# Wide fifth blocks and idle matmuls in a fused attention and feed-forward kernel

## The chip, the cores and the metric

The kernel runs on one core of a Trainium2 chip. The metric is the device time of one execution in microseconds; the time of a kernel is the median over several runs. A core has TensorE (PE, which takes a block of weights into its array and streams columns past it), VectorE (DVE), ScalarE (ACT), GpSimd (POOL) and SyncE (SP, which issues most DMAs). Each executes its own instructions in program order.

## The reference

Attention over 8 batches x 8 heads, 576 positions, 64 values per head, with a mask in blocks of 64 (a query sees keys of its own block and of earlier ones), followed by a feed-forward layer of 4608 tokens, 512 inputs and 2048 inner values, all in float32:

```python
scores = scale * np.matmul(q, k.transpose(0, 1, 3, 2))
scores = np.where(block_i >= block_j, scores, -1e9)
attn = softmax(scores)                      # row maximum taken off first
x = np.matmul(attn, v)                      # -> (4608, 512)
h = x @ w_in                                # 512 -> 2048
sp = np.maximum(h, 0.0) + np.log1p(np.exp(-np.abs(h)))
out = (h * erf(sp)) @ w_out                 # 2048 -> 512
```

## The kernel before, in words

Every float32 operand of a matmul is split into a float16 high part and a float16 low part, and products are sums of two or three float16 matmuls.

**A head n** (64 of them, batch after batch) goes through these steps. `load_qk` brings its keys and queries, `split_qk` makes their high and low parts and copies them by six DMAs into one of three tiles `qk` of 128 rows and 4 x 576 + 64 columns: four parts of 576 columns (part 0 keys low and high, 1 queries high and low, 2 keys high, 3 queries high), with rows of mask below. `maxes` computes scores `s` (L586) with blocks of 128 queries as weights and keys streaming past, and DVE takes each row's maximum (L590); PE transposes them (`mt`, L620) and a DMA puts them into the tile's row 68. `probs` computes the scores again the other way round, `t` (two matmuls, L638 and L639, into one PSUM bank), with blocks of 128 keys as weights and queries streaming past; ACT takes the exponential into `p32` (L643), and ACT, POOL and DVE split it into `ph` and `pl`. For each pair of heads, `pv` multiplies by the values (`u`, L686; 64 columns of weights a head) and `sums` adds up the rows (`us`, L715; 32 columns of ones). For every four heads, `normalise` turns the reciprocal sums (`rt`, L733; transposes `rb`, L751) and stores `x`.

576 is 4 x 128 + 64. The fifth block of queries in `maxes`, of keys in `probs`, `pv` and `sums`, and of positions in `normalise` therefore has 64 rows or columns, which appear as `r`, `kk` and `min(P, S - j * P)`. Rows 64 to 127 of the fifth block of `p32` are set to zero at the start, and the values `v` come padded with zeros to 640 rows.

**The feed-forward part** starts when the weights are decoded (`decode`, `measure_weights`, `split_weight`, on ACT and DVE, over about the first 200 us) and the first batch's `x` is there. A tile of 256 tokens takes four units; a unit is 48 matmuls of 256 columns (`m_h`, L431), a gate on ACT and DVE, and 24 matmuls of 512 columns (`o`, L446).

**The order.** All steps are tasks of a planner (`Plan`). A task has an engine, a cost in ns, the tasks it depends on, the PSUM or SBUF buffers it takes, and a priority: for a step of slot n roughly n plus a fraction (`merge`). The planner simulates the engines with these costs, always gives a free engine the ready task of the lowest priority, and the order that results is the program order of each engine. There are eight PSUM banks; a task that takes one waits in the plan until one is free. Matmuls on PE are booked with 0.4167 ns a column and a few ns.

**Idle matmuls.** `warm` adds a matmul of a constant onto a bank `b_w` that nobody reads. The list of slot n < 8 holds ten of them, with priority n + 1 to n + 2, so they come behind the slot's other work.

Of the kernel before, what the change touches and what calls it, by code (L numbers as in the profile page):

```python
# [22 lines left out]
DEC0, DECR, SPLIT = (0.5, 6.5), (0.35, 0.4), 0.8  # L23
MOE, STEP = 12.5, 0.93
NPH = 3
BYSUM = 4
PSUM = bass.MemoryType.PSUM

# [188 lines left out]
def tile_attention_moe(ctx: ExitStack, tc: tile.TileContext, qk, v, w, maskrows, sels, out):  # L217
    nc = tc.nc
    B, H, D2, S = qk.shape
# [3 lines left out]
    P = 128  # L223
# [9 lines left out]
    NB = 3  # L233
# [6 lines left out]
    NP = (2, 2)  # L240
    plan = Plan()
    add = plan.add
# [21 lines left out]
    ident = cpool.tile([P, P], F32, name="ident")  # L264
# [30 lines left out]
    def mmns(n, f16=False):  # L295
        return n * 0.4167 + (3 if f16 else 13)
# [162 lines left out]
    qks = [spool.tile([P, 4 * S + 64], F16, name=f"qk{i}") for i in range(NB)]  # L459
    for t in qks:  # L460
        nc.sync.dma_start(t[D : D + 5, 2 * S : 4 * S], maskrows)
    sel = spool.tile([P, 4], F32, name="sel")
    nc.sync.dma_start(sel, sels)

# [9 lines left out]
    ident16 = ident.bitcast(F16)[:, :P]  # L474
# [45 lines left out]
    def part(n, i):  # L520

        return qks[n % NB][:, i * S : (i + 1) * S]

    def Q(n, *names):
        return [("qk", n % NB, i) for i in names]

# [52 lines left out]
    def maxes(n):  # L579

        mx, K, hx = mxs[n % 2], D + 4, token("mx", 2)
        kh, qh = part(n, 2), part(n, 3)

        def mm(s, c0, i, k0, w_):
            r = min(P, S - i * P)
            add("PE", mmns(w_, True), lambda: nc.tensor.matmul(s()[:r, c0 : c0 + w_], lhsT=qh[:K, i * P : i * P + r], rhs=kh[:K, k0 : k0 + w_], start=True, stop=True),  # L586
                r=[*Q(n, "kh", "qh"), hx], w=[s])

        def red(col, s, c0, w_, r=P):
            add("DVE", 145 + 1.07 * w_, lambda: nc.vector.tensor_reduce(out=mx[:r, col : col + 1], in_=s()[:r, c0 : c0 + w_], axis=AX.X, op=ALU.max, negate=True),  # L590
                r=[s], w=[("mx", n % 2, col)])

        def a():
            s = bank(f"s01_{n}")
            mm(s, 0, 0, 0, 256)
            mm(s, 256, 1, 0, 256)
            red(0, s, 0, 128)
            red(1, s, 256, 256)

        def b():  # L600
            s = bank(f"s2_{n}")
            mm(s, 0, 2, 0, 384)
            red(2, s, 0, 384)

        def c():
            s = bank(f"s3_{n}")
            mm(s, 0, 3, 0, 512)
            red(3, s, 0, 512)

        def d(j):  # L610
            s = bank(f"s4_{n}_{j}")
            mm(s, 0, 4, 288 * j, 288)
            red(4 + j, s, 0, 288, 64)

        def e():
            add("DVE", 300, lambda: nc.vector.tensor_tensor(out=mx[:64, 4:5], in0=mx[:64, 4:5], in1=mx[:64, 5:6], op=ALU.min), r=[("mx", n % 2, 5)], w=[("mx", n % 2, 4)])

        def f():
            pt = bank(f"mt{n}")
            add("PE", 60, lambda: nc.tensor.transpose(out=pt()[:5, :P], in_=mx[:, :5], identity=ident), r=[("mx", n % 2, i) for i in range(6)] + [hx], w=[pt])  # L620
            mt = buf("a", [5, P], F16, "mt", f"mt_{n}")
            add("ACT", 255, lambda: nc.scalar.activation(mt(), pt()[:5, :P], AF.Copy, scale=1.0 / 32), r=[pt], w=[mt])
            add("ACT", 60, lambda: nc.scalar.dma_start(qks[n % NB][D + 4 : D + 5, 3 * S :].rearrange("o (i p) -> o i p", p=P), mt()), r=[mt], w=Q(n, "m"), lag=2500.0)

        return [a, b, c, lambda: d(0), lambda: d(1), e], f

    def probs(n, out):

        K = D + 5
        sc = qsc[n // 4]  # L630
        klh, qhl, kh, qh = [part(n, i) for i in range(4)]

        def one(j, q0, w_):
            kk = min(P, S - j * P)
            ks = slice(j * P, j * P + kk)
            s = bank(f"t{j}_{n}_{q0}")

            add("PE", mmns(w_, True), lambda: nc.tensor.matmul(s()[:kk, :w_], lhsT=klh[:, ks], rhs=qhl[:, q0 : q0 + w_], start=True, stop=False), r=Q(n, "kl", "kc", "ql", "qc", "m"), w=[s])  # L638
            add("PE", mmns(w_, True), lambda: nc.tensor.matmul(s()[:kk, :w_], lhsT=kh[:K, ks], rhs=qh[:K, q0 : q0 + w_], start=False, stop=True), r=Q(n, "kh", "qh", "m"), w=[s])  # L639
            skip = max(0, starts[j] - q0)  # L640
            pt, c = offs[j]
            c += q0 + skip - starts[j]
            add("ACT", 190 + 0.84 * (w_ - skip), lambda: nc.scalar.activation(p32s[pt][n % NP[pt]][:kk, c : c + w_ - skip], s()[:kk, skip:w_], AF.Exp, scale=sc()[:kk, 1:2]),  # L643
                r=[s, sc], w=[("p32", pt, n % NP[pt], j, q0)])

        def split(pt, keys):
            p = p32s[pt][n % NP[pt]]
            ph = buf("a", [P, PN[pt]], F16, f"ph{pt}", f"ph{pt}_{n}", NPH)
            pl = buf("a", [P, PN[pt]], F16, f"pl{pt}", f"pl{pt}_{n}", NPH)
            keys = [("p32", pt, n % NP[pt], *k) for k in keys]  # L650
            if pt:
                add("POOL", 1100, lambda: nc.gpsimd.tensor_copy(ph(), p), r=keys, w=[ph])  # L652
            else:
                add("ACT", 850, lambda: nc.scalar.copy(ph(), p), r=keys, w=[ph])
            eng, ns, on = (("DVE", 1250, nc.vector), ("POOL", 2050, nc.gpsimd))[pt]
            add(eng, ns, lambda: on.tensor_tensor(out=pl(), in0=p, in1=ph(), op=ALU.subtract), r=keys + [ph], w=[pl])  # L656
            out.append((ph, pl))

        return [lambda: one(0, 0, 288), lambda: one(0, 288, 288), lambda: one(3, 320, 256),
                lambda: (one(4, 320, 256), split(0, [(0, 0), (0, 288), (3, 320), (4, 320)])), lambda: one(1, 128, 448),  # L660
                lambda: (one(2, 256, 320), split(1, [(1, 128), (2, 256)]))]

    def pv(qd, pp, prs, V, usb, rs, krs):

        vsb, vh, vl = V
        def ranges(q0, q1):

            for j in range(5):
                if starts[j] < q1:
                    a = max(q0, starts[j])  # L670
                    pt, c = offs[j]
                    c += a - starts[j]
                    yield j, min(P, S - j * P), a - q0, pt, slice(c, c + q1 - a)

        def go(hf):
            q0, q1 = halves[hf]
# [46 lines left out]
    def normalise(b, qd, usbs, rs, krs):  # L723
# [14 lines left out]
        def m(pp):  # L738
            c = 2 * qd + pp
# [5 lines left out]
            for hf, (q0, q1) in enumerate(((0, 384), (384, 576))):  # L745
                rb = bank(f"rb{nm}_{pp}_{hf}")

                def mms(q0=q0, q1=q1, rb=rb):
                    for i in range(q0 // P, (q1 + P - 1) // P):
                        r = min(P, S - i * P)  # L750
                        nc.tensor.transpose(out=rb()[:, i * P - q0 : i * P - q0 + r], in_=rw()[:r, i].rearrange("p a b -> p (a b)"), identity=ident[:r, :r])  # L751

                add("PE", 330, mms, r=[(rw, hf)], w=[rb])
                w = q1 - q0
                add("DVE", 550 - 200 * hf, lambda q0=q0, q1=q1, rb=rb, w=w: nc.vector.tensor_tensor(out=rb()[:, :w], in0=usbs[pp]()[:, q0:q1], in1=rb()[:, :w], op=ALU.mult),
                    r=[(usbs[pp], 0), (usbs[pp], 1)], w=[rb])
                add("ACT", 500 - 160 * hf, lambda q0=q0, q1=q1, rb=rb, w=w: nc.scalar.copy(x16()[:, 0, q0:q1], rb()[:, :w]), r=[rb], w=[(x16, 0, hf)])
                add("DVE", 550 - 200 * hf, lambda q0=q0, q1=q1, rb=rb, w=w: nc.vector.tensor_tensor(out=x16()[:, 1, q0:q1], in0=rb()[:, :w], in1=x16()[:, 0, q0:q1], op=ALU.subtract),
                    r=[rb, (x16, 0, hf)], w=[(x16, 1, hf)])
# [5 lines left out]
    def merge(base, lists):  # L765

        order = []
        for n_, (steps, lo, hi, off) in enumerate(lists):
            order += [(lo + (hi - lo) * (i + 0.5) / len(steps), n_, i) for i in range(len(steps))]
        for p, n_, i in sorted(order):  # L770
            plan.prio = base + p + lists[n_][3]
            lists[n_][0][i]()
# [2 lines left out]
    vs, vs_, prs, usbs, rows = {}, {}, {}, {}, {}  # L775
    normals = {}
    NTT = NT // T
    WARM = 10
    NH = 2
    NO = 3  # L780
    PV = -1.2
# [45 lines left out]
    krs = {}  # L827
    b_w = bank("warm")

    def warm():  # L830
        add("PE", 220, lambda: nc.tensor.matmul(b_w(), lhsT=ident16, rhs=ident16[:, None, :].broadcast_to([P, 4, P]), start=True, stop=True), w=[b_w])

    for s in range(2):
        for f in range(NF):
# [10 lines left out]
    for slot in range(N + 4):  # L845
        n = slot
# [35 lines left out]
        if n in normals:  # L882
# [1 line left out]
            b, q_ = divmod(qd, NQ)  # L884
            js = (2 * qd, 2 * qd + 1)
            lists.append((normalise(b, q_, [usbs.pop(j) for j in js], [rss[j % 3] for j in js], [krs.pop(j) for j in js]), 0.6, 1, 0.0))
        if n < 8:
            lists.append(([warm] * WARM, 0, 1, 1.0))
        merge(n, lists)
        for t in range(NTT):  # L890
            if t not in x1 and ready(t) <= n + 1:
# [45 lines left out]
```

## Time and profile before

| | |
|---|---|
| median of 3 runs | 1317.13 us (1315.54 to 1319.36) |
| profiled execution | 1318.73 us, span 1316.8 us |
| PE busy | 1211.3 us (92%), 9334 matmuls |
| ACT busy | 936.9 us (71%) |
| DVE busy | 851.6 us (65%) |
| POOL busy | 176.8 us (13%) |
| mean granted TensorE clock | 0.926 |
| DMA | 104.42 MB, mean 79 GB/s |

Busy is the time in which at least one instruction of the engine ran. Matmuls overlap, so their durations add up to more than the time they need; the distance from one start to the next says what one costs. A row of a group is: line, engine, operation, output<-inputs, weights (rows*columns), streamed operand (rows x columns), count | busy us, mean ns of one | idle time of the engine before them and what ended it. A row in order of time is: start, duration (of all that are merged into it), engine, line, names, shapes, count, and in brackets the idle time before. A row of waits is: who waited <- for whom: us in total, times, longest. A row of the chain of waits is: start, us, engine and line, count.

### The profile page before, as it was taken

The page shows a single profiled execution, that of the slowest core. Times are in us where ns is not written, and L with a number is a line of the kernel's source. Part 1 is how long each engine was busy: PE and PEld are TensorE (multiplying, and loading weights), DVE is VectorE, ACT ScalarE, POOL GpSimd, SP SyncE. Part 2 cuts the span into 40 slices and gives each one's busy share as a digit, 9 for nine tenths or more (in the row PEclk, how much of TensorE's full clock was granted, in tenths as well). Part 3 has the DMA queues.
Part 4 walks back from the last instruction along what each step waited for, and adds up shares of the span by engine and source line. Part 5 has one row for each costly group of instructions (what it writes and reads, how often), then busy time and mean ns, then how long its engine had stood idle before and what let it go on. Part 6 is the DMA issues. An engine that isn't in the chain of part 4 may idle for free.

```text
span 1316.8 us, 23689 instructions
## 1 busy us (share of the span) xinstructions
PE 1211.3 (92%) x9334; PEld 770.2 (58%) x9334; DVE 851.6 (65%) x1689; ACT 936.9 (71%) x1517; POOL 176.8 (13%) x151
## 2 busy tenths in 40 slices
PE   8766667879999999999999999999999999999997
PEld 3333334456665656666665666666666666766664
DVE  4698688974767675866676666757676745443332
ACT  4677467786777667777666776867787777767775
POOL 0221120100111110112011111101111111000000
PEclk8666658889999989998998999999999999999999
DMA  6555561311313141223222141413221220011000
GB/s 228 148 187 173 167 161 44 85 34 58 107 39 98 41 136 40 82 64 96 74 77 79 43 119 30 120 26 108 71 80 48 78 54 25 17 51 33 17 17 16
DMA packets 80668, 104.42 MB, mean 79 GB/s; under 512 B 10399, under 2 KB 61599, under 8 KB 80558
## 3 DMA queue, kind: packets, MB, share of 16 engines
q1 hardware_dynamic: 69678, 93.39, 24.0%
q10 hardware_dynamic: 10880, 9.53, 3.1%
q8 instruction: 73, 1.20, 0.4%
q14 instruction: 37, 0.30, 0.1%
HBM read 55.61 MB, written 18.87 MB: 57 GB/s over the span
## 4 chain that ended last, share of the span: by engine, by line
PE 69%; ACT 5%; DVE 2%; DMA 2%; issue 1%; ACTq 1%; SPq 0%; DVEq 0%
PE o L446 25%; PE m_h L431 25%; PE u L686 4%; PE t L638 3%; PE s L586 3%; PE t L639 2%; ACT m_r L400 2%; PE us L715 2%; DMA qk<-qhi 1%; PE rb L751 1%; PE rt L733 1%; ACT p L643 1%; DVE m_r L404 0%; ACT m_gh L412 0%; ACT m_r L391 0%
## 5 line engine op out<-in xcount | busy, mean ns | idle before, releaser
L431 PE MATMUL m_h<-xh,wsb 128*128 128x256 f16 x2304 | 402.3, 275 | 4.1 <-DVE wsb L338 1.3
L431 PEld LDWEIGHTS <-wsb 128*128 128x128 f16 x3456 | 339.4, 99 | 59.5 <-issue 5.9
L400 ACT ACTIVATE m_r<-m_r,c 128x1024 f32<-128x1024 f32 x288 | 330.0, 1146 | 50.4 <-DVE m_r L404 31.6
L446 PE MATMUL o<-wsb,m_gh 128*128 128x512 f16 x1152 | 339.8, 386 | 11.2 <-ACT m_gh L412 11.1
L431 PE MATMUL m_h<-xl,wsb 128*128 128x256 f16 x1152 | 317.0, 275 | 0.0
L643 ACT ACTIVATE p<-t,qsc 128x288 f32<-128x288 f32 (+4 forms) x384 | 173.6, 479 | 116.9 <-PE t L639 111.1
L590 DVE TENSOR_REDUCE mx<-s 64x1 f32<-64x288 f32 (+4 forms) x384 | 167.4, 469 | 90.7 <-PE s L586 89.4
L446 PE MATMUL o<-wsb,m_gl 128*128 128x512 f16 x576 | 208.8, 383 | 0.0
L652 POOL CAST ph<-p 128x768 f16<-128x768 f32 x64 | 63.6, 994 | 947.0 <-ACT p L643 881.0
L404 DVE SCALAR_TENSOR_TENSOR m_r<-m_r,m_r 128x1024 f32<-128x1024 f32 x72 | 88.8, 1233 | 157.4 <-ACT m_r L400 157.3
L446 PEld LDWEIGHTS <-m_gh 128*128 128x128 f16 x1152 | 111.6, 99 | 132.0 <-ACT m_gh L412 16.0
L391 ACT ACTIVATE m_r<-m_h,c,bsc 128x512 f32<-128x512 f32 (+3 forms) x192 | 122.3, 670 | 38.3 <-PE m_h L431 37.7
L586 PE MATMUL s<-qk 68*128 68x256 f16 (+3 forms) x384 | 107.3, 350 | 38.0 <-DMA qk<-qhi 30.0
L639 PE MATMUL t<-qk 69*128 69x288 f16 (+4 forms) x384 | 125.3, 331 | 17.7 <-DMA qk<-mt 17.7
L638 PE MATMUL t<-qk 128*128 128x288 f16 (+4 forms) x384 | 126.4, 332 | 9.3 <-DVE mx L590 3.4
L411 DVE SCALAR_TENSOR_TENSOR m_h<-m_r,m_h 128x512 f32<-128x512 f32 x144 | 92.7, 688 | 40.8 <-ACT m_r L400 40.3
L656 POOL TENSOR_TENSOR pl<-p,ph 128x768 f16<-128x768 f32 x64 | 111.0, 1734 | 5.1
L412 ACT CAST m_gh<-m_h 128x512 f16<-128x512 f32 x144 | 81.5, 584 | 31.1 <-DVE m_h L411 28.8
L413 DVE TENSOR_TENSOR m_gl<-m_h,m_gh 128x512 f16<-128x512 f32 x144 | 92.9, 681 | 11.8 <-ACT m_gh L412 10.5
L446 PEld LDWEIGHTS <-m_gl 128*128 128x128 f16 x576 | 56.5, 99 | 64.4 <-issue 4.4
L586 PEld LDWEIGHTS <-qk 68*128 68x128 f16 (+1 forms) x384 | 37.5, 109 | 88.0 <-issue 36.8
L638 PEld LDWEIGHTS <-qk 128*128 128x128 f16 (+1 forms) x384 | 41.1, 107 | 78.5 <-issue 56.2
(102 smaller groups left out, 1356.9 us busy)
## 6 DMA issues: line engine op xcount, KB each, us to landing
st<-qk SPq DMA_DIRECT2D x64, 288.0 KB
raw<-w SPq DMA_DIRECT2D x32, 512.0 KB
v<-v SPq DMA_DIRECT2D x16, 640.0 KB
qk<-qhi SPq DMA_DIRECT2D x128, 72.0 KB
qk<-qhi ACTq DMA_DIRECT2D x128, 72.0 KB
qk<-qlo SPq DMA_DIRECT2D x128, 72.0 KB
x_d<-x SPq DMA_DIRECT2D x32, 288.0 KB
out<-ob SPq DMA_DIRECT2D x36, 256.0 KB
```

The lines of the kernel that those rows point to most:

```text
L391: add("ACT", 310 + 0.84 * w * (y - x) / T, lambda i=i, h=h, b=b, x=x, y=y, w=w: nc.scalar.activation(cut(br[0]()[:, i * w : (i + 1) * w], ...
L400: add("ACT", 300 + 0.834 * UW, lambda r=r, a=a, pp=pp: nc.scalar.activation(r(), a(), AF.Square, bias=const(pp[1]), scale=pp[0]), r=[a] + ...
L411: add("DVE", 690, lambda cs=cs, h=h: nc.vector.scalar_tensor_tensor(out=h(), in0=r()[:, cs], scalar=end, in1=h(), op0=ALU.add, op1=ALU.mul ...
L413: add("DVE", 690, lambda cs=cs, h=h: nc.vector.tensor_tensor(out=bgl()[:, cs], in0=h(), in1=bgh()[:, cs], op=ALU.subtract), r=ks[i] + [(bg ...
L431: nc.tensor.matmul(hk(k), lhsT=wf16(0, f, lo)[:, cc * P : (cc + 1) * P], rhs=x()[:, cc, :], start=cc == 0 and i == 0, stop=cc == NCC - 1 a ...
L446: nc.tensor.matmul(o[c](), lhsT=a()[:, sl], rhs=wf16(1, f, wlo), start=u == 0 and k == 0 and not lo and wlo == 0, stop=u == NU - 1 and k = ...
L586: add("PE", mmns(w_, True), lambda: nc.tensor.matmul(s()[:r, c0 : c0 + w_], lhsT=qh[:K, i * P : i * P + r], rhs=kh[:K, k0 : k0 + w_], star ...
L590: add("DVE", 145 + 1.07 * w_, lambda: nc.vector.tensor_reduce(out=mx[:r, col : col + 1], in_=s()[:r, c0 : c0 + w_], axis=AX.X, op=ALU.max, ...
L638: add("PE", mmns(w_, True), lambda: nc.tensor.matmul(s()[:kk, :w_], lhsT=klh[:, ks], rhs=qhl[:, q0 : q0 + w_], start=True, stop=False), r= ...
L639: add("PE", mmns(w_, True), lambda: nc.tensor.matmul(s()[:kk, :w_], lhsT=kh[:K, ks], rhs=qh[:K, q0 : q0 + w_], start=False, stop=True), r= ...
L643: add("ACT", 190 + 0.84 * (w_ - skip), lambda: nc.scalar.activation(p32s[pt][n % NP[pt]][:kk, c : c + w_ - skip], s()[:kk, skip:w_], AF.Ex ...
L656: add(eng, ns, lambda: on.tensor_tensor(out=pl(), in0=p, in1=ph(), op=ALU.subtract), r=keys + [ph], w=[pl])
```

## The change

Two things. First, the fifth blocks use 128 rows or columns of weights: `maxes` and `probs` take their weights through `wide`, which reads 640 columns from a part's start (beyond part 3 lie the 64 spare columns of the tile, now set to zero by a memset at the start; beyond parts 0 and 2 lie the first 64 columns of the next part), and `pv`, `sums` (through `ranges`) and the transposes of `normalise` take all 128 rows. What is read out of the results stays the same. Second, the 80 old idle matmuls stand in the lists of the first two slots (40 each) instead of the first eight, and slots 1 to 13 get 50 further ones each, of 256 columns, which the plan books at 150 ns and places after the first exponential of head n - 1.

```diff
+FILL, FILLS = 14, 50
...
     for t in qks:
         nc.sync.dma_start(t[D : D + 5, 2 * S : 4 * S], maskrows)
+        nc.gpsimd.memset(t[:, 4 * S :], 0.0)
...
+    def wide(n, i):
+        return qks[n % NB][:, i * S : i * S + 5 * P]
...   # maxes
-        kh, qh = part(n, 2), part(n, 3)
+        kh, qh = part(n, 2), wide(n, 3)
-            r = min(P, S - i * P)
-            ... nc.tensor.matmul(s()[:r, c0 : c0 + w_], lhsT=qh[:K, i * P : i * P + r], ...
+            ... nc.tensor.matmul(s()[:, c0 : c0 + w_], lhsT=qh[:K, i * P : i * P + P], ...
...   # probs
-        klh, qhl, kh, qh = [part(n, i) for i in range(4)]
+        klh, qhl, kh, qh = wide(n, 0), part(n, 1), wide(n, 2), part(n, 3)
-            ks = slice(j * P, j * P + kk)
+            ks = slice(j * P, j * P + P)
-            ... nc.tensor.matmul(s()[:kk, :w_], lhsT=klh[:, ks], ...
+            ... nc.tensor.matmul(s()[:, :w_], lhsT=klh[:, ks], ...
...   # pv, sums
-                    yield j, min(P, S - j * P), a - q0, pt, slice(c, c + q1 - a)
+                    yield j, P, a - q0, pt, slice(c, c + q1 - a)
...   # normalise
-                        r = min(P, S - i * P)
-                        nc.tensor.transpose(out=rb()[:, i * P - q0 : i * P - q0 + r], in_=rw()[:r, i]..., identity=ident[:r, :r])
+                        nc.tensor.transpose(out=rb()[:, i * P - q0 : i * P - q0 + P], in_=rw()[:, i]..., identity=ident)
...
-    WARM = 10
+    WARM = 40
...
-    def warm():
-        add("PE", 220, lambda: nc.tensor.matmul(b_w(), lhsT=ident16, rhs=ident16[:, None, :].broadcast_to([P, 4, P]), start=True, stop=True), w=[b_w])
+    def warm(n=None):
+        w = 4 if n is None else 2
+        t = add("PE", 220 if n is None else 150, lambda: nc.tensor.matmul(b_w()[:, : w * P], lhsT=ident16, rhs=ident16[:, None, :].broadcast_to([P, w, P]), start=True, stop=True), w=[b_w])
+        if n is not None:
+            t.deps.add(plan.written["p32", 0, (n - 1) % NP[0], 0, 0])
...
-        if n < 8:
+        if n < 2:
             lists.append(([warm] * WARM, 0, 1, 1.0))
+        if 0 < n < FILL:
+            lists.append(([lambda n=n: warm(n)] * FILLS, 0, 1, 1.0))
```

More of the change, by code (lines that the diff above doesn't have):

```diff
@@ L581, in maxes @@
         mx, K, hx = mxs[n % 2], D + 4, token("mx", 2)
-        kh, qh = part(n, 2), part(n, 3)
+        kh, qh = part(n, 2), wide(n, 3)
         def mm(s, c0, i, k0, w_):
-            r = min(P, S - i * P)
-            add("PE", mmns(w_, True), lambda: nc.tensor.matmul(s()[:r, c0 : c0 + w_], lhsT=qh[:K, i * P : i * P + r], rhs=kh[:K, k0 : k0 + w_], start=True, stop=True),
+            add("PE", mmns(w_, True), lambda: nc.tensor.matmul(s()[:, c0 : c0 + w_], lhsT=qh[:K, i * P : i * P + P], rhs=kh[:K, k0 : k0 + w_], start=True, stop=True),
                 r=[*Q(n, "kh", "qh"), hx], w=[s])
@@ L630, in probs @@
         sc = qsc[n // 4]
-        klh, qhl, kh, qh = [part(n, i) for i in range(4)]
+        klh, qhl, kh, qh = wide(n, 0), part(n, 1), wide(n, 2), part(n, 3)
         def one(j, q0, w_):
             kk = min(P, S - j * P)
-            ks = slice(j * P, j * P + kk)
+            ks = slice(j * P, j * P + P)
             s = bank(f"t{j}_{n}_{q0}")
-            add("PE", mmns(w_, True), lambda: nc.tensor.matmul(s()[:kk, :w_], lhsT=klh[:, ks], rhs=qhl[:, q0 : q0 + w_], start=True, stop=False), r=Q(n, "kl", "kc", "ql", "qc", "m"), w=[s])
-            add("PE", mmns(w_, True), lambda: nc.tensor.matmul(s()[:kk, :w_], lhsT=kh[:K, ks], rhs=qh[:K, q0 : q0 + w_], start=False, stop=True), r=Q(n, "kh", "qh", "m"), w=[s])
+            add("PE", mmns(w_, True), lambda: nc.tensor.matmul(s()[:, :w_], lhsT=klh[:, ks], rhs=qhl[:, q0 : q0 + w_], start=True, stop=False), r=Q(n, "kl", "kc", "ql", "qc", "m"), w=[s])
+            add("PE", mmns(w_, True), lambda: nc.tensor.matmul(s()[:, :w_], lhsT=kh[:K, ks], rhs=qh[:K, q0 : q0 + w_], start=False, stop=True), r=Q(n, "kh", "qh", "m"), w=[s])
             skip = max(0, starts[j] - q0)
@@ L749, in mms @@
                     for i in range(q0 // P, (q1 + P - 1) // P):
-                        r = min(P, S - i * P)
-                        nc.tensor.transpose(out=rb()[:, i * P - q0 : i * P - q0 + r], in_=rw()[:r, i].rearrange("p a b -> p (a b)"), identity=ident[:r, :r])
+                        nc.tensor.transpose(out=rb()[:, i * P - q0 : i * P - q0 + P], in_=rw()[:, i].rearrange("p a b -> p (a b)"), identity=ident)
                 add("PE", 330, mms, r=[(rw, hf)], w=[rb])
```

## The prediction

> **What bounds the kernel now.** I read the page's slices first, then a table by stage, then PE's groups and its order in time in the late stage, then who waits for whom in the early stage.
>
> ```profile
> span 1316.8 us, 23689 instructions
> ...
> PE 1211.3 (92%) x9334; PEld 770.2 (58%) x9334; DVE 851.6 (65%) x1689; ACT 936.9 (71%) x1517; POOL 176.8 (13%) x151
> ...
> PE   8766667879999999999999999999999999999997
> PEclk8666658889999989998998999999999999999999
> ```
>
> From the tenth slice on (33 us each) PE is at 9 or more; before that it is at 6 to 8, and the granted clock is at 5 or 6 in slices two to six. So there are two stages with two limits, and the diff has one half for each: the wide fifth blocks concern PE's own time, the idle matmuls the clock. The table by stage (length, then busy time of PE, PEld, DVE, ACT, POOL, then granted clock, DMA share, GB/s) puts numbers on it:
>
> ```profile
> 33.00:198.00 165.00, 109.11 (x780) 57.63 (x779) 131.63 (x292) 105.78 (x221) 36.46 (x26) 0.61 0.57 167
> 198.00:303.00 105.00, 84.53 (x606) 51.46 (x607) 86.02 (x164) 79.89 (x127) 12.27 (x8) 0.87 0.20 51
> 303.00:1157.00 854.00, 838.06 (x6822) 549.36 (x6820) 562.19 (x1120) 627.86 (x1015) 125.87 (x94) 0.99 0.25 70
> 1157.00:1317.00 160.00, 152.49 (x1029) 100.67 (x1026) 56.03 (x75) 109.51 (x131) 0.00 (x0) 0.99 0.08 26
> ```
>
> From 303 to 1157 us PE is busy for 838 of 854 us at a clock of 0.99, ACT for 628, DVE for 562: PE is the limit there, and an instruction that takes less of PE is worth its time. From 33 to 198 us PE is busy for only 109 of 165 us although its clock is 0.61, and DVE is the fullest engine (132). After 1157 us only the feed-forward part is left, which the diff leaves alone.
>
> **The change, part 1: wide fifth blocks.** The sequence is 576 = 4 x 128 + 64, so the fifth block has 64 rows or columns. The diff touches it in five places; here is how often each comes in the late stage (46 heads; a few records are missing):
>
> ```profile
> L586 PE MATMUL s<-qk 68*64 68x288 f16 x89 | 27.0, 305 | 3.6 <-DVE mx L590 2.9 <-ACT p L643 0.3 <-ACT ob L805 0.2
> L638 PE MATMUL t<-qk 128*64 128x256 f16 x46 | 13.6, 296 | 0.0
> L751 PE MATMUL rb<-ident,rw 64*128 64x64 f32 x26 | 7.1, 272 | 0.0
> L686 PE MATMUL u<-ph,vh 64*64 64x64 f16 x48 | 5.2, 213 | 0.0
> L715 PE MATMUL us<-ph,ones 64*32 64x64 f16 x48 | 4.9, 199 | 0.0
> ```
>
> These durations hide what counts, since matmuls overlap. The cost is the distance from one start to the next, in the order in time:
>
> ```profile
> 594.48 0.35 PE L639 MATMUL t<-qk 69*128 69x448 f16 x1
> 594.76 0.31 PE L586 MATMUL s<-qk 68*64 68x288 f16 x1
> 595.00 0.27 PE L548 MATMUL qt<-ident,qm 128*1 128x128 f32 x1
> ...
> 601.22 0.30 PE L639 MATMUL t<-qk 69*128 69x320 f16 x1
> 601.36 0.29 PE L638 MATMUL t<-qk 128*128 128x288 f16 x1
> 601.49 0.29 PE L639 MATMUL t<-qk 69*128 69x288 f16 x1
> ...
> 648.13 0.38 PE L586 MATMUL s<-qk 68*128 68x512 f16 x1
> 648.44 0.30 PE L638 MATMUL t<-qk 128*64 128x256 f16 x1
> 648.57 0.28 PE L639 MATMUL t<-qk 69*64 69x256 f16 x1
> 648.72 0.28 PE L586 MATMUL s<-qk 68*64 68x288 f16 x1
> ```
>
> Between wide neighbours the step is the column count: 320 columns from 601.22 to 601.36 (0.14 us), 288 to 601.49 (0.13), about 0.43 ns a column. From a wide matmul into a 64-wide one it is longer: 448 columns should take 0.19 and take 0.28 (594.48 to 594.76), 512 should take 0.22 and take 0.31 (648.13 to 648.44): +0.09 each. On the way out, 288 columns should take 0.12 and take 0.24 (594.76 to 595.00): +0.12. Between two 64-wide ones there is little (+0.02 from 648.44, +0.04 from 648.57). So a stretch of 64-wide weights costs 0.21 us, and wide weights stream the same columns in the same time without it.
>
> Score blocks s: two per head, 92 x 0.21 = 19.3 us. Blocks t: 46 x (0.09 in, 0.02 between, 0.10 out) = 9.7. In the order in time I count 24 t that stand directly before an s and share one way out and in: minus 24 x 0.19, plus 24 x 0.04 = -3.6. Together 25.4; listing all such steps gives 23 with the records that are there, and I take 24.
>
> ```profile
> 599.03 0.49 PE L751 MATMUL rb<-ident,rw 128*128 128x128 f32 x3
> 599.36 0.27 PE L431 MATMUL m_h<-xh,wsb 128*128 128x256 f16 x1
> 600.67 0.47 PE L751 MATMUL rb<-ident,rw 128*128 128x128 f32 x2
> 601.08 0.31 PE L638 MATMUL t<-qk 128*128 128x320 f16 x1
> ...
> 608.62 0.26 PE L715 MATMUL us<-ph,ones 128*32 128x192 f16 x4
> 608.70 0.25 PE L715 MATMUL us<-pl,ones 128*32 128x192 f16 x4
> 608.88 0.20 PE L715 MATMUL us<-ph,ones 64*32 64x64 f16 x2
> ...
> 641.49 0.25 PE L686 MATMUL u<-ph,vl 128*64 128x192 f16 x2
> 641.58 0.25 PE L686 MATMUL u<-pl,vh 128*64 128x192 f16 x2
> 641.75 0.22 PE L686 MATMUL u<-ph,vh 64*64 64x64 f16 x2
> ```
>
> Transposes rb: three wide ones take 0.33 (599.03 to 599.36), so 0.11 each; one wide and one of 64 rows (merged in the row at 600.67) take 0.41. Wide they would take 0.22: 26 x 0.19 = 4.9 us, with the doubled columns paid. Output products u: the step into 64 rows is 0.17 where the one before was 0.09, +0.08 to 0.09; 24 pairs of heads give 2.1 us. Sums us: 0.18 against 0.08, +0.10 x 24 = 2.4. The way out of u and us stays, because 64- or 32-column weights remain there. Sum: 24 + 4.9 + 2.1 + 2.4 = 33 us of PE time in the late stage.
>
> How much of it arrives at the end: PE idles 16 us there now, and with 33 us less to do it will meet data that isn't ready more often; ACT would be busy for 628 of about 825 us, so no engine takes over as a whole. The ends are 20 (the waits nearly double) and 33; nearest to the row with 98% busy is the upper one, and I take 28.
>
> The Trainium skill (TensorEngine Tiling (Array Packing), Tiling Modes) has a rule against this edit: small tiles run independently, two at once, and widening gives that up. By it, the two 64-wide s of a head could share one streaming time, and 46 x 0.12 = 5.5 us of this would be forgone, an estimate that leaves 27 of the 33. The trace does not show them at once: at 594.76 one of them runs alone between two wide ones.
>
> The other costs of part 1: three memsets on POOL at the start (POOL 13% busy), nothing. No wait is new: the extra 64 columns are those of tiles on which the same step already waits, and half-used weights load beside the matmuls (PEld 549 of 854 us).
>
> **Part 2: idle matmuls.** The 80 old ones stay 80: they depend on nothing, all ran by 33 us (none after, below), and stand there as before. New are 13 x 50 = 650 of 256 columns. In the planned order those of slot n come after the first exponential of head n-1 and behind that slot's own work; the plan books 150 ns for each. On the chip nothing holds them: PE runs them in order when it reaches them, and what is behind them (scores for DVE's maxima L590, t for ACT's exponentials L643) waits.
>
> ```profile
> 33.00:198.00 165.00, 0.00 (x0) 0.00 (x0) 0.61 0.57 167
> ...
> 128.80 0.42 PE L638 MATMUL t<-qk 128*128 128x256 f16 x1
> 129.01 0.42 PE L639 MATMUL t<-qk 69*128 69x256 f16 x1
> ...
> 302.72 5.24 PE m_h L431 x48
> ...
> PE s L586 <- DMA qk<-qhi: 23.0, 7, 6.7
> PE t L639 <- DMA qk<-mt: 17.7, 8, 4.7
> ...
> DVE mx L590 <- PE s L586: 11.1, 5, 5.9
> DVE usb L694 <- PE u L686: 4.7, 4, 1.4
> DVE qsc L566 <- PE qb L562: 3.4, 1, 3.4
> ```
>
> A matmul of 256 columns takes 5.24/48 = 0.109 us at the full clock (302.72, chain of waits) and 0.21 at the low one (128.80 to 129.01). So the fill is 71 us of PE at the full clock. PE's own work there, 109 us at 0.61, is 67 at the full clock: 138 of 165 us, and it fits if the clock is at least 138/165 = 0.84. Today PE idles 56 of 165 us, mostly in the waits for DMA (7 for 23 us, the longest 6.7; 8 for 17.7). Filled, PE is at over eight tenths, and the page's slices with 9 have the clock at 9. So I expect 0.85 to 0.95.
>
> The Trainium skill (TensorE: Matmul & The Clock Gate, Part 1) says one idle window of about 3.4 us drops the clock to half and one busy window restores it. By that about five long DMA waits would cost two windows each, 34 us at half clock: 0.90, an estimate on the same side of 0.84; the trace, at 0.61 with waits of 6.7 and 4.7 us, agrees so far.
>
> What is it worth? DVE is the fullest engine (132 of 165) and waited on PE for 19 us in the three rows above; a PE at 0.9 instead of 0.61 shortens that by a third, 6 us. Bounds: all 19 gone, and 4 more in later slots; or -10, when PE, now four fifths full with work that can't be skipped, is late where it was early. I take +5, nearest to the third. The fill's PSUM bank stays taken for 170 us longer, so seven are left; PE's waits in the early stage name DMA, not readers of banks, so nothing, with 7 us as the upper end. What is late next is DVE and the SP queue behind it.
>
> **Sum.** 28 + 5 = 33 us. The profiled execution took 1318.7 (span 1316.8); it becomes 1285.7. It was 1.6 over the median of the three runs, 1317.1, so against that: 1284.
>
> **Rivals.**
> First, the clock pays in full: DVE's waits on PE vanish and the late stage passes on 30: 1317 - 30 - 23 = 1264. For it: at 0.61 PE's work takes 1.6 times as long as it must. Against: DVE at 80%, and DMA waits that no clock shortens.
> Second, the fill is neutral or costs up to 15, being late in front of real work: 1317 - 28 + 0 to 15, middle 1297.
> Third, the other side: the clock does not rise, so each filler takes 0.21 and the first thirteen heads become bound by PE. At 0.61, 138/0.61 = 226 us for what took 165: +61 - 28, 1350. It ends slower when 138/c exceeds 165 + 28, below a clock of 0.72. For it: in slice two PE is at 7 and the clock still at 6. Against: with the fill, PE has no slice at 6.
> Fourth, the 33 us turn into waits: heads come at the pace of the keys' and queries' DMA, 1310. Against: 16 us of idle in 854.
>
> **How the numbers follow.** Forecast 0.56; first rival 0.18; second 0.16; third 0.05; fourth 0.05. The likeliest one's own range is 1276 to 1292. The range for all is 1263 to 1302: it takes in the first and second rivals and leaves out the third, the fourth and some of the ends. This kernel's runs spread by 0.3% (1315.5 to 1319.4), which is about what can be told from no change. Faster by more: forecast, first, second and part of the fourth, 0.92. Same: 0.03. Slower: 0.05.
>
> **What would show it.** Right: no PE group of 64 columns or rows of weights but u's 128*64 and us's 128*32; the step before the fifth block equals its columns; about 6822 matmuls of the late stage in 25 us or more less; the granted clock from 33 to 198 us over 0.84 with PE at 9; head 13's first exponential (L643) some 5 us earlier; DVE's waits on L586 shorter. Wrong: a clock below 0.75 with PE full early; PE's idle time in the late stage over 35 us; idle matmuls after 303 us, each 0.109 us off the gain.

## The result and the profile after

The changed kernel takes 1273.5 us (median; 1272.6 to 1274.1) against 1318.2 for the kernel before beside it: a ratio of 0.9662, 95% interval 0.9643 to 0.9681, 45 us less. A second set gave 0.9663 (0.9645 to 0.9680). The forecast was 1284, range 1263 to 1302: the result lies in the range, under the forecast's own 1276 to 1292 and about halfway to the first rival's 1264.

The page of the changed kernel, with the same rows as before, and the slices of GB/s left out:

```profile
span 1271.7 us, 25003 instructions
...
PE 1199.7 (94%) x9984; PEld 834.3 (66%) x9984; DVE 852.4 (67%) x1689; ACT 935.4 (74%) x1517; POOL 177.2 (14%) x154
...
PE   5898899789999989999999999999999999999997
PEclk7899999889999999998999999999999999999999
```

Slices two to six had PE at 6 or 7 and the clock at 5 or 6; now they have 8 or 9 and 8 or 9. The tables by stage are cut at a fixed piece of work: the seventh feed-forward unit (unit 6), which started at 314.7 us before and starts at 305.7 now, and at unit 60, when attention is over, 1177.2 and 1132.1. First before, then after (length, busy PE, PEld, DVE, ACT, POOL, clock, DMA share, GB/s):

```profile
33.00:314.70 281.70, 205.28 (x1460) 116.59 (x1460) 220.81 (x461) 193.52 (x358) 48.73 (x34) 0.72 0.41 119
314.70:1177.20 862.50, 846.62 (x6881) 555.42 (x6881) 566.14 (x1125) 633.90 (x1021) 125.87 (x94) 0.99 0.25 70
1177.20:1316.80 139.60, 132.28 (x889) 87.12 (x887) 48.92 (x65) 95.62 (x115) 0.00 (x0) 0.99 0.06 20
```

```profile
33.00:305.70 272.70, 240.49 (x2152) 176.12 (x2152) 222.94 (x465) 194.05 (x357) 47.98 (x35) 0.94 0.41 121
305.70:1132.10 826.40, 809.33 (x6877) 563.03 (x6877) 563.53 (x1116) 630.94 (x1019) 126.70 (x94) 0.99 0.26 74
1132.10:1271.70 139.60, 132.23 (x889) 87.14 (x887) 48.89 (x65) 95.78 (x115) 0.00 (x0) 0.99 0.06 20
```

The early stage is 9 us shorter, the middle one 36, the last one the same to 0.1 us. In the middle PE has the same matmuls (6881 and 6877) and is busy 37 us less, while its idle time stays at 16 to 17 us. The early figure is soft: a second profile of the same kernel has unit 6 at 311.1, 5 us later, and the whole 6 us longer. Medians of runs decide there, not one profile. The forecast's sign of head 13 is as soft (its first exponential was to come some 5 us earlier): that starts at 203.6 us before, at 194.0 in this profile, at 201.0 in the second, and at 198.9 with the wide blocks alone.

The steps that carried the forecast, in order of time, in the changed kernel (lines have moved: s is L591, t L643 and L644, u L691, us L720, rb L755):

```profile
632.70 0.35 PE L644 MATMUL t<-qk 69*128 69x448 f16 x1
632.89 0.29 PE L591 MATMUL s<-qk 68*128 68x288 f16 x1
633.01 0.30 PE L643 MATMUL t<-qk 128*128 128x320 f16 x1
...
612.05 0.20 PE L720 MATMUL us<-ph,ones 128*32 128x64 f16 x2
612.08 0.20 PE L720 MATMUL us<-pl,ones 128*32 128x64 f16 x2
612.21 0.30 PE L591 MATMUL s<-qk 68*128 68x288 f16 x1
...
619.46 0.25 PE L691 MATMUL u<-pl,vh 128*64 128x192 f16 x2
619.54 0.20 PE L691 MATMUL u<-ph,vh 128*64 128x64 f16 x2
...
101.00 0.71 PE L755 MATMUL rb<-ident,rw 128*128 128x128 f32 x5
101.54 0.27 PE L625 MATMUL mt<-ident,mx 128*5 128x128 f32 x1
```

448 columns to the fifth block take 0.19 us (0.28 before), its 288 columns 0.12 (0.24 before). Into the last 64 rows of u it is 0.08 (0.17), and five transposes of a head pair take 0.54, 0.11 each. The way out of us (612.08 to 612.21, 0.13 for a pair of 64 columns) is still paid, as the forecast said.

### The profile page after: what moved, and what is told of

It is laid out like the page before. It is cut to its first block, busy times and chain, and to the rows that moved or that the text cites. A ratio compares the mean times of both kernels' runs of the same rounds, so it can differ in the third digit from the quotient of the medians.

```text
span 1271.7 us, 25003 instructions
## 1 busy us (share of the span) xinstructions
PE 1199.7 (94%) x9984; PEld 834.3 (66%) x9984; DVE 852.4 (67%) x1689; ACT 935.4 (74%) x1517; POOL 177.2 (14%) x154
## 4 chain that ended last, share of the span: by engine, by line
PE 69%; ACT 6%; DVE 2%; issue 1%; DMA 1%; ACTq 1%; DVEq 0%
PE m_h L432 27%; PE o L447 26%; PE u L691 4%; ACT m_r L401 3%; PE s L591 3%; PE t L643 3%; PE t L644 2%; PE us L720 2%; ACT p L648 1%; PE rt L738 1%; PE rb L755 1%; DMA qk<-qhi 1%; DVE m_r L405 1%; ACTq L583 0%; DVE m_h L412 0%
## 5 line engine op out<-in xcount | busy, mean ns | idle before, releaser
L591 PE MATMUL s<-qk 68*128 68x256 f16 (+3 forms) x384 | 96.4, 314 | 28.9 <-DMA qk<-qhi 22.4
L643 PE MATMUL t<-qk 128*128 128x288 f16 (+3 forms) x384 | 114.5, 303 | 6.7 <-DVE mx L595 2.4
L644 PE MATMUL t<-qk 69*128 69x288 f16 (+3 forms) x384 | 114.5, 304 | 2.5 <-DMA qk<-mt 2.5
L836 PE MATMUL warm<-ident 128*128 128x256 f16 (+1 forms) x730 | 111.8, 289 | 1.5 <-POOL ident masks.py:199 1.5
L836 PEld LDWEIGHTS <-ident 128*128 128x128 f16 x730 | 71.8, 99 | 23.5 <-issue 2.5
```

Of the source, the lines that this page charges most:

```text
L591: add("PE", mmns(w_, True), lambda: nc.tensor.matmul(s()[:, c0 : c0 + w_], lhsT=qh[:K, i * P : i * P + P], rhs=kh[:K, k0 : k0 + w_], start ...
L643: add("PE", mmns(w_, True), lambda: nc.tensor.matmul(s()[:, :w_], lhsT=klh[:, ks], rhs=qhl[:, q0 : q0 + w_], start=True, stop=False), r=Q( ...
L644: add("PE", mmns(w_, True), lambda: nc.tensor.matmul(s()[:, :w_], lhsT=kh[:K, ks], rhs=qh[:K, q0 : q0 + w_], start=False, stop=True), r=Q( ...
L836: t = add("PE", 220 if n is None else 150, lambda: nc.tensor.matmul(b_w()[:, : w * P], lhsT=ident16, rhs=ident16[:, None, :].broadcast_to( ...
```

## The experiments

Each is compared with the kernel before run on the same chip. "Unit 6" is the start of the seventh feed-forward unit in its profile; clock is that from 33 to 198 us.

| kernel | median us | ratio (95%) | clock | unit 6, us |
|---|---|---|---|---|
| before | 1316 to 1318 | 1 | 0.61 | 314.7 |
| changed | 1273.5 | 0.9662 (0.9643 to 0.9681) | 0.97 | 305.7 |
| changed, again | 1272.2 | 0.9663 (0.9645 to 0.9680) | 0.93 | 311.1 |
| fill alone | 1317.0 | 1.0000 (0.9982 to 1.0019) | 0.94 | 317.1 |
| wide alone | 1278.6 | 0.9714 (0.9687 to 0.9740) | 0.63 | 310.3 |
| changed, fill cut to 2 columns | 1278.2 | 0.9709 (0.9690 to 0.9729) | 0.69 | 310.9 |
| wide scores alone | 1287.9 | 0.9778 (0.9754 to 0.9802) | 0.65 | 307.3 |
| changed, 25 a slot | 1290.8 | 0.9803 (0.9784 to 0.9822) | 0.86 | 314.1 |
| changed, 90 a slot | 1319.9 | 1.0013 (0.9995 to 1.0031) | 0.94 | 353.1 |
| fill alone, 25 a slot | 1326.5 | 1.0079 (1.0058 to 1.0099) | 0.83 | 323.5 |
| changed, every second idle matmul | 1274.9 | 0.9673 (0.9636 to 0.9709) | 0.82 | 309.8 |
| 25 a slot, cut to 2 columns | 1285.1 | 0.9747 (0.9711 to 0.9782) | 0.70 | 309.7 |
| changed, fill of 192 columns | 1275.8 | 0.9672 (0.9629 to 0.9715) | 0.95 | 299.4 |
| narrow, fill cut to 2 columns | 1320.9 | 1.0024 (0.9999 to 1.0048) | 0.66 | 317.6 |

**The two halves, one at a time.** Fill alone: the changed kernel with the narrow blocks of before.

```diff
-            ... nc.tensor.matmul(s()[:, c0 : c0 + w_], lhsT=qh[:K, i * P : i * P + P], ...
+            ... nc.tensor.matmul(s()[:r, c0 : c0 + w_], lhsT=qh[:K, i * P : i * P + r], ...
...   # and kk rows or columns again in probs, pv, sums and normalise
```

> The 650 idle matmuls alone, with the narrow fifth blocks of before. Theory A (two independent parts: the fill raises the clock early and is worth about 10 us, the wide blocks save shape switches in the late stage): 7 to 12 us faster than before, about 1308; granted clock over 0.9 from 33 to 198 us; feed-forward unit 6 about 9 us earlier than before, and nothing more gained from there to the end. Theory B (the early gain comes from the wide blocks, which switch shapes at half clock there): 0 to 3 us faster. Theory C (the late stage gains more than its switches because the fill's order carries on): 15 us or more faster.

Measured: nothing, 1.0000. The clock did rise to 0.94, and no time came of it. Of the three theories only B, with 0 to 3 us, has room for this; A and C fall. B stands or falls with the next run.

Wide alone: the changed kernel without the 650 new idle matmuls, the old 80 as before.

```diff
-        if 0 < n < FILL:
-            lists.append(([lambda n=n: warm(n)] * FILLS, 0, 1, 1.0))
```

> The wide fifth blocks alone, the 80 old idle matmuls as before and no new ones; the plan has the same costs as before and so the same order. Theory A: 32 to 36 us faster, about 1284, with unit 6 at most 3 us earlier than before and the clock from 33 to 198 us still near 0.6. Theory B: 42 us or more faster, unit 6 about 9 us earlier. Theory C: 25 to 30 us faster.

Measured: 0.9714, 38 us less. It falls between theories A (32 to 36) and B (42 or more), and so does unit 6, which comes 4.4 us earlier: none of the three has both runs right. From there the stage with attention and feed-forward work together shrinks by 34.5:

```profile
33.00:310.30 277.30, 199.87 (x1456) 124.72 (x1456) 219.42 (x456) 192.47 (x356) 47.81 (x34) 0.71 0.41 118
310.30:1138.30 828.00, 809.55 (x6883) 561.57 (x6881) 565.65 (x1125) 630.97 (x1021) 127.06 (x94) 1.00 0.26 73
```

So the wide blocks carry 38 of the 45 us, and the fill brings the rest only in their company.

**The fill without its time.** The 650 new matmuls have 2 columns; the plan books them at 150 ns all the same, so all other work keeps the changed kernel's order.

```diff
-nc.tensor.matmul(b_w()[:, : w * P], lhsT=ident16, rhs=...)
+nc.tensor.matmul(b_w()[:, :2], lhsT=ident16, rhs=ident16[:, :2], ...)      # new ones only
```

> The changed kernel with the 650 new matmuls cut to 2 columns each; the plan still books 150 ns for each, so the order of all other work is that of the changed kernel, and only the filled time is missing. If the fill works through the clock: clock from 33 to 198 us near 0.6, unit 6 within 3 us of before, time as with the wide blocks alone, about 1284. If it works through the changed order (or the wide blocks): time within 3 us of the changed kernel's 1273, whatever the clock.

Measured: 1278.2, the time of the wide blocks alone, at a clock of 0.69. This is the first branch, but for details (unit 6 is 3.8 us earlier than before, not within 3): with wide blocks this order with its short matmuls is worth nothing, and the full length of the fill on it is worth 0.9709 - 0.9662, 6 us. The short matmuls are not free:

```profile
105.94 0.34 PE L836 MATMUL warm<-ident 128*128 128x2 f16 x8
106.14 0.30 PE L643 MATMUL t<-qk 128*128 128x320 f16 x1
```

Eight take 0.20 us, so all 650 take some 16 us of PE at the full clock, an estimate. This control has about a quarter of the fill's time, not none of it.

**How much of the wide blocks.** Wide alone, with narrow rows again in values, sums and transposes:

```diff
-                    yield j, P, a - q0, pt, slice(c, c + q1 - a)
+                    yield j, min(P, S - j * P), a - q0, pt, slice(c, c + q1 - a)
...   # and in_=rw()[:r, i], identity=ident[:r, :r] in normalise
```

> Wide fifth blocks in the two score steps only (s and t); values, sums and transposes keep their 64 rows, no new idle matmuls. By the sum of steps: 24 of the 33 us of PE time in the late stage, so 22 to 27 us faster than before, about 1293, and 8 to 10 us slower than with all blocks wide. If rows of 64 (transposes, values, sums) weigh more than their steps said, the distance to all blocks wide is 13 us or more; if they cost nothing at the end, under 5 us.

Measured: 1287.9, 28 us less than before and 9.3 more than with all blocks wide. The division into 24 for the scores and 9 for the rest holds roughly; the total is larger than the sum of steps, because the early stage and the clock have a part in it (below).

**How much fill.** These three were to tell whether the fill is paid in PE time.

```diff
-FILL, FILLS = 14, 50
+FILL, FILLS = 14, 25      # 90 in the second; 25 and narrow blocks in the third
```

> The changed kernel with 25 instead of 50 idle matmuls in each of slots 1 to 13 (325 instead of 650). Theory P (the fill is paid in PE time: with it PE idles only 31 of 273 us up to feed-forward unit 6, so what the clock gives the fill takes): half the fill takes 35 us less of PE; the clock from 33 to 198 us falls to 0.8 to 0.9, and the time is 1 to 6 us under the changed kernel's. Theory Q (the fill runs in gaps and is free, and what is left is set by DVE and DMA): same as the changed kernel if the clock stays over 0.9, up to 5 us slower if it falls to 0.8.

> The changed kernel with 90 instead of 50 idle matmuls a slot: 520 more, 57 us of PE at the full clock. Theory P: PE has 31 us of idle time to take them, so at least 20 us slower, 1293 or more, and the first feed-forward units move back by as much. Theory Q: within 4 us of 1273, clock over 0.95.

> 25 idle matmuls a slot with the narrow fifth blocks of before (50 of them made no difference to before). Theory P: the filled PE also pays for each change of weights' shape in the first heads, and half the fill relieves it: 3 to 8 us faster than before, about 1311. Theory Q: no difference to before, within 3 us, or slower.

Measured: 90 a slot is 47 us slower than 50. That is what theory P had:

```profile
33.00:353.10 320.10, 295.49 (x2669) 226.17 (x2668) 224.54 (x460) 197.07 (x359) 46.09 (x35) 0.96 0.36 104
```

PE is busy 295 of 320 us, DVE still has 225 us of work as in every other kernel, and all of it takes 47 us longer than the changed kernel's 272.7: the 520 further ones are 57 us of PE, and PE had 32 us of idle time before unit 6, of which 25 are left. Once PE is full, each further idle matmul delays real work. (The plan's order is another one here too; that part was not run by itself.) But 25 a slot should then have been faster than 50, and it was 18 us slower, and with narrow blocks 9 us slower than before. With wide blocks both theories fell; with narrow ones "or slower" of theory Q is met, without a reason for it. The planner was the suspect: other tasks in the plan mean another order on every engine.

The order was held fixed in one kernel, with every second of the 50 tasks emitting nothing:

```diff
-            lists.append(([lambda n=n: warm(n)] * FILLS, 0, 1, 1.0))
+            lists.append(([lambda n=n, i=i: warm(n, i % 2) for i in range(FILLS)], 0, 1, 1.0))   # only odd ones emit
```

and the order of 25 a slot was run without its time in another (`FILLS = 25` and the 2 columns above):

> The changed kernel's plan and order (50 new tasks a slot, 150 ns each), but only every second one emits its idle matmul of 256 columns: 325 run. It has the fill time of the kernel with 25 a slot and the order of the changed one. If the 18 us that 25 a slot lost lay in its other order (theory O): 1270 to 1278, between the changed kernel and its tiny fill. If they lay in the clock that half a fill no longer holds (theory K): 1286 or more, clock from 33 to 198 us at 0.86 as there.

> The plan with 25 new tasks a slot, whose matmuls are cut to 2 columns: the order of the kernel with 25 a slot, without its fill. Theory O: as slow as with the fill or a few us slower, 1290 to 1296, although the order's only difference to the changed kernel are tasks that take no time. Theory K: near the wide blocks alone, 1275 to 1281.

Measured: 1274.9 with 325 idle matmuls in the changed kernel's order, as theory O had it; 1285.1 with 325 of 2 columns in the order of 25 a slot, between the two theories. So theory O holds in part: with the same number of idle matmuls the time differs by 16 us with the order that the plan makes around them (1290.8 against 1274.9), and 7 us of it stay without the fill's time (1285.1 against 1278.2). The loss of that order lies partly where no idle matmul stands any more. Its middle stage, first with 2 columns in the order of 25, then with 2 columns in the changed kernel's order:

```profile
309.70:1145.30 835.60, 816.96 (x6882) 565.63 (x6881) 566.30 (x1123) 631.22 (x1020) 126.98 (x94) 0.99 0.26 73
...
PE s L591 <- DMA qk<-qhi: 4.6, 6, 2.3
PE s L591 <- DVE mx L595: 4.1, 4, 1.7
```

```profile
310.90:1136.70 825.80, 809.54 (x6876) 563.42 (x6876) 564.05 (x1116) 630.21 (x1019) 126.64 (x94) 0.99 0.26 74
...
PE s L591 <- DVE mx L595: 1.7, 1, 1.7
PE s L591 <- DMA qk<-qhi: 1.1, 1, 1.1
```

It is 10 us longer with the same matmuls. PE is busy 7 us longer: the trace has the clock at half for 24 us there against 10, which costs about half of the 14. PE waits 6 us more for keys and maxima, but less for others: in all its idle time is 2 us more (18.6 against 16.3). In that order the fill of 25 then costs 7 us more (0.9803 against 0.9747) instead of bringing any; why is open.

**Less time for each.** In the changed kernel's order:

```diff
-nc.tensor.matmul(b_w()[:, : w * P], lhsT=ident16, rhs=...)
+nc.tensor.matmul(b_w()[:, :192], lhsT=ident16, rhs=ident16[:, None, :64].broadcast_to([P, 3, 64]), ...)   # new ones only
```

> The changed kernel's plan and order with its 650 new matmuls at 192 instead of 256 columns: 53 instead of 71 us of PE at the full clock. If the clock stays over 0.9 and what the fill takes from PE counts: 1 to 5 us under the changed kernel, about 1269. If the fill is free where it stands: within 2 us of 1272. If the clock falls under 0.85: 1274 to 1278.

Measured: 0.9672 (0.9629 to 0.9715), with runs from 1264.6 to 1280.5. Inconclusive: the clock of 0.95 rules out the third branch, and the other two lie within the spread. The profile shown in the table is of the fastest run. With the order fixed, the ratios are 0.9709 at 2 columns, 0.9673 at half the matmuls, 0.9672 at three quarters of the columns, 0.9662 at the whole. With so little between the last three no dose better than the changed one is shown, and the intervals at half and at three quarters reach up to that of the 2 columns.

**Why the fill alone gave nothing.** The fill alone, its new matmuls cut to 2 columns by the edit shown above:

> Narrow fifth blocks with the changed kernel's plan and the new matmuls cut to 2 columns, to see why the fill alone gave nothing. If the clock is worth 5 us with narrow blocks as well and the new order cost it: 1321 to 1325, slower than before. If the order costs nothing and the filled PE pays for the narrow blocks' changes of shape what the clock gives: 1314 to 1319, no difference to before.

Measured: 1.0024 (0.9999 to 1.0048), between the two branches. It may be that with narrow blocks, too, the fill's time is worth a little (1.0024 to 1.0000) and the order costs about as much; the intervals overlap, and neither is shown. What the trace adds is the price of narrow blocks between idle matmuls, in the fill alone:

```profile
102.09 0.60 PE L838 MATMUL warm<-ident 128*128 128x256 f16 x4
102.62 0.30 PE L644 MATMUL t<-qk 128*64 128x256 f16 x1
102.75 0.27 PE L645 MATMUL t<-qk 69*64 69x256 f16 x1
102.96 0.28 PE L838 MATMUL warm<-ident 128*128 128x256 f16 x1
```

Four idle matmuls, 0.44 us, take 0.53 before a narrow block, and the second narrow one takes 0.21 for 256 columns: the same 0.09 in and 0.10 out as late. In a PE with 76 us of idle time up to unit 6 (before, 281.7 less 205.3) such steps can fall into waits. In a filled one there is less room for that:

```profile
33.00:317.10 284.10, 257.29 (x2151) 172.92 (x2151) 223.66 (x465) 194.55 (x357) 47.97 (x34) 0.92 0.40 116
```

That is the fill alone, 27 us of idle time. Less idle time and less what the half clock took (half of PE's busy time in the stretches in which the trace has the clock at 0.5), PE's stretch from 33 us to unit 6 is 239 us in the fill alone and 228 in the changed kernel, 11 apart; without fill, 153 before and 146 with the wide blocks alone, 7 apart. So the narrow blocks' steps cost more in company of the fill, by 4 us. That accounts for a part of the 7 us by which the two halves together (45) exceed their sum (38 and 0); the rest is open, and the start of unit 6, which differs by 5 us between two profiles of the changed kernel, can't settle it.

## Why the prediction was right, and where not

**The steps of the late stage: right.** Forecast were 33 us of PE time from shape changes. Taking out idle time and what the half clock cost, PE's middle stage went from 835 to 805 us (changed) and 806 (wide alone): 29 to 31 us. With wide scores alone it is 815:

```profile
307.30:1144.70 837.40, 821.21 (x6881) 562.22 (x6881) 565.93 (x1125) 631.93 (x1021) 126.95 (x94) 0.99 0.26 73
```

So the division over scores and the rest, 24 and 9 in the forecast, is 21 and 8 to 10.

**How much of it arrives: the term that was mis-sized.** The forecast let 28 of 33 us through, with 33 as the upper end, because PE would wait more. The middle stage shrank by 36 us, 34.5 with the wide blocks alone. Of the 36 us, 31 are less work, 6 are less half clock, and 1 is lost again to waits. So nearly all of the steps' time arrived: PE's idle time there grew by 1 to 3 us, not 5. And the time at half clock, which the working had left out of this stage, fell as well: in the trace 24 us of this stage are at half clock before, 10 after and 7 with the wide blocks alone, worth 11, 5 and 3 us of PE's time. Two stretches show it; before:

```profile
462.00:495.00 33.00, 30.09 (x209) 19.21 (x210) 24.00 (x53) 23.38 (x39) 4.93 (x4) 0.90 0.48 129
693.00:726.00 33.00, 30.95 (x244) 19.41 (x243) 22.58 (x41) 22.77 (x36) 4.61 (x4) 0.90 0.28 73
```

and after:

```profile
462.00:495.00 33.00, 29.68 (x249) 20.16 (x247) 21.67 (x47) 22.86 (x39) 2.46 (x2) 0.95 0.34 96
693.00:726.00 33.00, 32.62 (x275) 23.47 (x273) 22.66 (x43) 23.35 (x39) 5.32 (x4) 1.00 0.13 33
```

Before, the clock falls at 483.5 us, in a wait of 2.3 us for keys (from 481.7). But with the wide blocks alone PE waits 2.2 us at the same place of the order, and the clock stays up:

```profile
474.43 0.55 PE L591 MATMUL s<-qk 68*128 68x256 f16 x3 [2.19 <-DMA qk<-qhi]
...
462.00:495.00 33.00, 30.11 (x260) 20.51 (x258) 25.38 (x55) 24.35 (x39) 5.25 (x4) 1.00 0.48 134
```

What decides it is not shown. These 6 to 8 us were in no term of the sum; that the range had room for them is luck.

**Wide blocks in the early stage: a term put at nothing.** The forecast counted the shape changes of 46 heads, after 303 us, and gave the early ones no value. With the wide blocks alone PE has 7 us less to do up to unit 6 (153 to 146), and unit 6 starts 4.4 us earlier.

**The fill: the size was right by luck, and in part it came another way.** +5 us were forecast, as a term of its own beside that of the wide blocks. With narrow blocks the fill brought nothing, as in the second rival; with wide ones 6 us were found between the changed kernel and its 2-column fill. The clock rose to 0.97, above 0.84 as it had to, so the third rival (a clock that stays low) fell. But the way was to be DVE's shorter waits on PE, above all those of the maxima. Single waits got shorter (the longest 2.8 us, 5.9 before), but there are more of them, and their total rose:

```profile
DVE mx L595 <- PE s L591: 13.6, 18, 2.8
DVE qsc L572 <- PE qb L568: 1.1, 2, 0.7
...
DVE usb L699 <- PE u L691: 0.2, 1, 0.2
...
PE s L591 <- DMA qk<-qhi: 12.7, 9, 2.7
PE t L644 <- DMA qk<-mt: 2.5, 1, 2.5
```

18 waits for 13.6 us against 5 for 11.1; for the copies of u and the scales it is 0.2 and 1.1 (4.7 and 3.4 before). The three rows together fall from 19.2 to 14.9 us, not to nothing as the first rival had it. PE's own waits for DMA fell from 41 to 15 us, and idle matmuls now stand where it waited. The step "it fits if the clock is at least 0.84" was right: 50 a slot fit, and 90 cost 47 us.

**A reading of the plan that was wrong.** The old 80 idle matmuls were to stand as before, all ahead of 33 us. In the changed kernel 40 of them do:

```profile
0.00:33.00 33.00, 10.34 (x40) 0.73 0.77 247
33.00:198.00 165.00, 96.38 (x652) 0.97 0.56 167
198.00:303.00 105.00, 5.04 (x40) 0.89 0.18 50
```

All idle matmuls write one bank, and the planner lets each wait for the one added before it. The second slot's 40 are mixed with new ones that wait for the first exponential, and run from 39 to 62 us. They are 40 x 0.216 = 9 us more of fill than was counted; the clock falls at 14.9 us instead of 22.7, without a visible price at head 0, whose first exponential starts at 34.6 us (36.7 before).

**What was left out.** That the two halves are not additive, and that the number of tasks in a plan changes the order of everything: the cost of an idle matmul was put at its PE time, while 25 instead of 50 a slot moved the whole by 18 us the wrong way. The forecast has no term for the new order. That this order costs nothing with wide blocks (1278.2 against 1278.6) is a measurement; nothing in the working argued for it, and here it was luck.

## What to carry to other kernels

Read PE's cost from start to start, not from durations: there a narrow block of weights between wide ones shows as 0.2 us that no row of a group has, and padding it to full size, with zeros or with columns whose results nobody reads, cost nothing that these runs show where the streamed columns stayed the same. Before filling gaps to lift the clock, compare the fill plus the real work at the full clock with the time there is; beyond that each filler is a delay (90 a slot), and a clock near 1 is no gain by itself (0.94 with the fill alone, at the same time as before). Where a planner makes the order, test a change of its task list with the work taken out (tasks booked, nothing emitted), or the order's chance is taken for the change's effect.

## What the runs showed of the hardware

At the full clock, a change from weights of 128 to weights of 64 columns cost about 0.09 us on the way in and 0.10 to 0.12 on the way out, with every neighbour looked at (feed-forward, scores, idle matmuls), and little between two narrow ones (0.02 to 0.04). From 128 to 64 rows of weights the way in cost 0.08 to 0.10. The Trainium skill (TensorEngine Tiling (Array Packing), Tiling Modes) says that changing the tiling mode drains TensorE; these steps agree, and it states no figure; that a drain is what takes the time, no run here shows. The granted clock was lifted from 0.61 to 0.97 in the first 200 us by 650 matmuls whose result nobody reads, and to 0.82 by half as many. A matmul of 2 columns still took 0.025 us from start to start.
